# An expert mixture between attention and a gated feed-forward: row-number transfers and the widening of 64-bit weights take other places

## Chip, cores and metric

The kernel runs on one core of a Trainium2 chip. The metric is the time of one execution in device microseconds; three runs of the kernel before are given.

## Reference

The output is three stages, one behind the other, all in single precision (two of the weight arrays of the third stage arrive as 64-bit floats, because their set-up divides by a 64-bit square root).

```python
def reference(q, k, v, w_gate, w1, w2, x2_gate, x2_val, x2_out, rms_g):
    x = causal_attention(q, k, v)          # 2 x 12 heads, 448 x 64 each
    x = x.reshape(896, 768)                # tokens x model
    # 8 experts with room for 112 tokens each; token-expert pairs are taken
    # in the order of falling logits x @ w_gate until every token has a place
    for e in range(8):
        h = np.maximum(x[mask_e] @ w1[e], 0.0)     # 768 -> 1024
        y[mask_e] = h @ w2[e]                      # 1024 -> 768
    rms = np.sqrt(np.mean(y * y, axis=-1, keepdims=True) + 1e-06)
    xn = y / rms * rms_g
    g = xn @ x2_gate                               # 768 -> 1536
    return (g / (1 + np.exp(-g)) * (xn @ x2_val)) @ x2_out
```

## The kernel before, in words

Attention works head by head and leaves the tokens as rows of a DRAM tensor `xs`. Then come eight routing rounds, each of which fixes one expert and its 112 tokens (class `Round`), and eight expert iterations (class `Expert`), in which a routing round for a later expert is worked in between. Behind them stands the feed-forward stage, in 12 chunks of 128 hidden units (line 779), and the output product with the scatter to token order (lines 798 to 849).

**Order of the work.** The expert part is written out by hand: strings of two-letter words (`ITER`, `LASTR`, `END`), which `emit` turns into instructions. Inside `tc.manual_schedule` TensorE, ScalarE, VectorE and GpSimd each keep the order of these words. SP is not in that list, and neither are the instructions behind the block: a planner puts them where it takes their engine and buffers to be free, also between those of the block. In a round r the words mean:

- U0 to U7 and D0 to D7: the up and down matmuls of the expert with weight chunks 16r to 16r+15 (lines 656, 691); A: relu of half the hidden units (`hs`, ScalarE); T and H: their transposes and the copy `hf` on ScalarE (line 681)
- X0, X1: transposes of the gathered tokens of the next expert and the copies `xf` on ScalarE (line 609)
- N0, N1, N2: square (`sq`) and root on ScalarE, reciprocal on VectorE, and the scaled rows `yn` on VectorE (line 705), of the expert before; Y0, Y1: their transposes and the splits `xnh`, `xnl`
- Q2', F0', F1': the next expert's number goes to a register of SP (line 492), its row numbers `idx` are computed (line 508) and its tokens are gathered by an indirect transfer on GpSimd's queue (line 511)
- C: widening of half a block of 64-bit weights, 128 x 384, to single precision: one operation on ScalarE (line 527) and five on VectorE (531 to 535); J: its split into `hi` (ScalarE, 539) and `lo` (VectorE, 540)
- K0 to K7: the gate and value matmuls of feed-forward chunk 0 (line 551); S: its sigmoid-weighted unit

**Buffers and loads.** All weight loads go through SP's queue, 384 KB each. Expert chunk m lies in one of three rings of nine buffers, by m mod 3: "hi", "lo", "raw". The 64-bit loads (`load64`) take "raw" buffers, the split pairs `hi` and `lo` take those two rings. `g64` and `t64`, the scratch of the widening, have three buffers each. `split(n)` loads up to chunk n + 18; chunks of an expert can only be loaded once its number is in SP's register.

**The row numbers.** The output scatter (line 820) needs the row numbers `idx` in another layout, `idt`. They go to DRAM and back in two transfers of 896 elements of 4 bytes, issued from ScalarE's queue and written down behind the hand-ordered block (lines 760, 762). ScalarE's queue is in order.

Of the kernel before, what the change touches and what calls it, by code (L numbers as in the profile page):

```python
# [10 lines left out]
U32 = mybir.dt.uint32  # L11
# [9 lines left out]
NT = 7  # L21
D = 768
E = 8
CAP = N // E
F1 = 1024
# [12 lines left out]
AHEAD = 18  # L38
START0 = 'M0 M1 G G'
START1 = "G1' G' P0' P1' G' P2' P3' P4' G' P5' G1' P6' Q0' Q1' M1 O' G F0' F1' G P0 P1 Q2' G G G P2 P3 G X0 P4 P5 G X1 P6 U0+ Q0 U1+ U2+ Q1 U3+ U4+ O"  # L40
ITER0 = "Y1 A0 M1 N2 U5 G F0' G T0 U6 Q2' F1' H0 U7 Y0 G G G D0 N1 P0 P1 A1 P2 T1 D1 D2 D3 G H1 P3 D4 G X0 D5 P4 P5 P6 N0 D6 Q0 X1 D7"
ITER = "U0 Q1' U1 N0 N1 N2 U2 U3 Q2' A0 M1 Y0 U4 O' Y1 G U5 F0' T0 U6 F1' H0 U7 A1 G D0 G P0 G P1 T1 D1 D2 G P2 H1 P3 G D3 D4 G D5 P4 P5 D6 P6 X0 D7 Q0 X1"
LASTR = 'U0 U1 N0 N1 N2 U2 U3 A0 Y0 Y1 U4 T0 U5 U6 U7 H0 D0 A1 T1 D1 D2 H1 D3 C0 D4 C1 D5 D6 J0 C2 D7 J1 C3 K0'
PRE = 1
GVP = (128, 128, 128, 128)
END = 'N0 N1 N2 K1 J2 J3 Y0 Y1 S0 K2 K3 K4 K5 K6 S1 K7'
RACT = (0, 1)
QK = 'dd'
VH = 'a'
# [26 lines left out]
def tile_attn_moe_ffn(ctx, tc, qk, v, consts, wts, wgv, wout, rmsg, out):  # L76
    nc = tc.nc

    keep = ctx.enter_context(tc.tile_pool(name="keep", bufs=1))
# [4 lines left out]
    def bank(tag, name, bufs=2):  # L84
        return pools["ps"].tile([128, 512], F32, tag=tag, name=name, bufs=bufs)
# [5 lines left out]
    idxd = dram.tile([N, 1], U32, name="idxd")  # L91
# [276 lines left out]
    gone = rt1.tile([128, E], F32, name="gone")  # L368
    nc.gpsimd.memset(gone, 0.0)
    idx = keep.tile([CAP, E], U32, name="idx")  # L370

    def weave(*chains):
        chains = list(chains)
        while chains:
            chains = [c for c in chains if next(c, True) is None]

    class Round:
# [122 lines left out]
        def F(self, c):  # L500
            if c == 0:
                self.pi = bank("r", "pi")
                for t in range(NT):
                    nc.tensor.matmul(self.pi[:CAP, :2], self.o[:, t, :], ids[:, t, :], start=(t == 0),
                                     stop=(t == NT - 1))
                return
            rd = self.rd
            nc.vector.tensor_scalar(idx[:, rd:rd + 1], self.pi[:CAP, :1], self.pi[:CAP, 1:2], float(N - 1),
                                    op0=ALU.add, op1=ALU.min)
            xg = ex.tile([CAP, D], F32, tag="xg", name="xg", bufs=2)  # L510
            nc.gpsimd.indirect_dma_start(out=xg, out_offset=None, in_=xs,  # L511
                                         in_offset=bass.IndirectOffsetOnAxis(ap=idx[:, rd:rd + 1], axis=0))
            xgs.append(xg)

    evs, xgs, raws, ready = [], [], [], []

    def half64(src, j):
        return src[j // 4, j // 2 % 2, :, j % 2 * 384:j % 2 * 384 + 384]

    def load64(src):  # L520
        raw = ring.tile([128, 384, 2], U32, tag="raw", name="w64", bufs=NR)
        nc.sync.dma_start(out=raw, in_=src.bitcast(U32).rearrange("p (a b) -> p a b", b=2))
        return raw

    def widen(raw):
        g = cv.tile([128, 384], F32, tag="g64", name="g64", bufs=3)
        nc.scalar.activation(g, raw[:, :, 1].bitcast(F32), AF.Copy, scale=2.0 ** -112)  # L527
        gu = g.bitcast(U32)
        t = cv.tile([128, 384], U32, tag="t64", name="t64", bufs=3)
        x = t.bitcast(F32)  # L530
        nc.vector.tensor_scalar(t, gu, 3, None, op0=ALU.logical_shift_left)
        nc.vector.scalar_tensor_tensor(t, gu, 0x80000000, t, op0=ALU.bitwise_and, op1=ALU.bitwise_or)  # L532
        nc.vector.tensor_scalar(gu, t, 0xFF800000, None, op0=ALU.bitwise_and)
        nc.vector.scalar_tensor_tensor(g, raw[:, :, 0], 2.0 ** -52, g, op0=ALU.mult, op1=ALU.mult)  # L534
        nc.vector.tensor_add(x, x, g)  # L535
        return x
# [7 lines left out]
    def gate_val(half, which, dcs):  # L544
        c0 = half * S
        wh, wl = early[which]
        if (half, which) not in gv0:
            gv0[half, which] = bank("a" if half else "r", "pg")
        for dc in dcs:
            for n, (w, x) in enumerate(((wh, xnh), (wh, xnl), (wl, xnh))):  # L550
                nc.tensor.matmul(gv0[half, which][:, :S], w[:, dc * 128:dc * 128 + 128], x[:, dc, c0:c0 + S],  # L551
                                 start=(dc == 0 and n == 0), stop=(dc == 5 and n == 2))

    def tiles64():
        return (ring.tile([128, 768], F32R, tag="hi", name="hi", bufs=NH),
                ring.tile([128, 768], F32R, tag="lo", name="lo", bufs=NH))

    early, wide, raws64 = [], [], []

    def native(r, c):  # L560
        return c in FULL.get(r, FULL[-1])

    def load(n):
        while len(raws) <= min(n, 16 * len(evs) - 1):
            while len(raws64) < len(GVP) and GVP[len(raws64)] <= len(raws):
                raws64.append(load64(half64(wgv, len(raws64))))
            r, c = divmod(len(raws), 16)
            home = HOMES[len(raws) % len(HOMES)]
            raw = ring.tile([128, 768], F32, tag=home, name="raw", bufs=NR if home == "raw" else NH)
            nc.sync.dma_start(out=raw, in_=wts[bass.ds(evs[r], 1), c].rearrange("o p f -> (o p) f"))  # L570
            raws.append(raw)

    def split(n):
        load(n + AHEAD)
        while len(ready) <= min(n, len(raws) - 1, 16 * E - 1):
            r, c = divmod(len(ready), 16)
            raw = raws[len(ready)]
            if native(r, c):
                ready.append((raw, None))
                continue  # L580
            hi = ring.tile([128, 768], F32R, tag="hi", name="hi", bufs=NH)
            lo = ring.tile([128, 768], F32R, tag="lo", name="lo", bufs=NH)
            nc.scalar.copy(hi, raw)
            pool = c not in LOV.get(r, LOV[-1])
            (nc.gpsimd if pool else nc.vector).tensor_sub(lo, raw, hi.bitcast(F32))
            ready.append((hi, lo))
# [132 lines left out]
    def emit(words, r0):  # L719
        for w in words.split():  # L720
            op, c, r = w[0], int(w[1:].rstrip("'+") or 0), r0 + w.count("+")
            if op in "MGPQ" or op in "OF":
                k = r + 2 - (w[-1] == "'")
                if 0 <= k < E:
                    getattr(rounds[k], op)(c)
            elif op == "K":
                half, which, part = c // 4, c // 2 % 2, c % 2
                gate_val(half, which, range(3 * part, 3 * part + 3))
            elif op == "S":
                sg0[c] = cv.tile([128, S], F32, tag="sg", name="sg", bufs=2)  # L730
                nc.scalar.activation(sg0[c], gv0[c, 0][:, :S], AF.Silu)
            elif op == "C":
                while len(raws64) <= c:
                    raws64.append(load64(half64(wgv, len(raws64))))
                wide.append(widen(raws64[c]))
            elif op == "J":
                if c % 2 == 0:
                    early.append(tiles64())
                hi, lo = early[c // 2]
                c0 = c % 2 * 384  # L740
                halves(wide[c], hi[:, c0:c0 + 384], lo[:, c0:c0 + 384])
            elif op == "X":
                if r + 1 < E:
                    if c == 0 and r >= 0:
                        exps.append(Expert(r + 1))
                    getattr(exps[r + 1], op)(c)
            elif op in "NY":
                if r > 0:
                    getattr(exps[r - 1], op)(c)
            else:  # L750
                getattr(exps[r], op)(c)

    ET = mybir.EngineType
    with tc.manual_schedule(engines={ET.PE, ET.Activation, ET.DVE, ET.Pool}):
        emit(START0, -2)
        emit(START1, -1)
        for r in range(E):
            emit(ITER0 if r == 0 else LASTR if r == E - 1 else ITER, r)
        emit(END, E)
    nc.scalar.dma_start(out=idxd.rearrange("(e p) o -> p (e o)", p=CAP), in_=idx)  # L760
    idt = keep.tile([128, NT], U32, name="idt")
    nc.scalar.dma_start(out=idt, in_=idxd.rearrange("(t p) o -> p (t o)", p=128))

    ectx.close()
    with ExitStack() as fctx:
# [13 lines left out]
        for fc in range(NFC):  # L779
            gh, gl = early[2 * fc] if fc < PRE else pair64(wgv[fc, 0])  # L780
            vh, vl = early[2 * fc + 1] if fc < PRE else pair64(wgv[fc, 1])
            for half in range(2):
# [60 lines left out]
        for t, g in ((4, "d"), (5, "r"), (6, "c")):  # L843
            o = pair(g)
# [61 lines left out]
```

## Time and profile before

| What | Value |
|---|---|
| Median of three runs | 624.35 us (624.24, 624.35, 626.61) |
| Profiled execution, its time | 622.68 us |
| Profiled execution, its span | 620.9 us |
| TensorE busy | 584.1 us (94%) |
| VectorE busy | 410.9 us (66%) |
| ScalarE busy | 237.9 us (38%) |
| Mean granted clock of TensorE | 0.977 |

The profile is one execution; its span goes from the first instruction to the last, and 1.78 us of its time lie outside. PE stands for TensorE, PEld for its weight loads, DVE for VectorE, ACT for ScalarE, POOL for GpSimd and SP for the engine that issues the loads; a q behind a name is the engine's sequencer or queue. L760 is line 760 of the kernel. The granted clock is a share of 2.4 GHz. A matmul's end is modelled and overlaps the next one's start.

### The profile page before, as it was taken

To read this page: it belongs to the slowest core of one execution; us is meant where nothing else is said; L and a number is where in the kernel's file an instruction comes from. 1 tells how busy PE (TensorE), PEld (TensorE's weight loads), DVE (VectorE), ACT (ScalarE), POOL (GpSimd) and SP (SyncE) were. 2 spreads that over 40 slices of the span, in tenths; PEclk is the share of its full clock that TensorE was granted. 3 is DMA by queue.
4 is the path that set the end of the run, shared out by engine and by line. 5 is a ranking of instruction groups with operands and counts; after the bars stand their busy time and mean duration, and the time that the engine had idled before them with its cause. 6 is when DMAs were issued, how large, how long until landed. Compare 5 with 4: busy or idle time off the path is not lost.

```text
span 620.9 us, 9817 instructions
## 1 busy us (share of the span) xinstructions
PE 584.1 (94%) x3336; PEld 480.9 (77%) x3336; DVE 410.9 (66%) x1175; ACT 237.9 (38%) x575; POOL 109.5 (18%) x101
## 2 busy tenths in 40 slices
PE   4899999749999999999879899999999999999995
PEld 3899999636666666666445699999999999999995
DVE  7799999795454464544201999999999982991410
ACT  5799998301222131221212544334444333341200
POOL 4677884220020220202000000000000000000210
PEclk9999999958999999999998999999999999999999
DMA  9988971119995957859693544444445450100210
GB/s 275 268 254 255 257 217 33 30 46 383 355 322 209 365 195 272 298 189 369 238 272 99 179 125 160 149 132 122 154 153 153 120 151 11 51 2 1 101 42 35
DMA packets 49793, 109.26 MB, mean 176 GB/s; under 512 B 17056, under 2 KB 19232, under 8 KB 49744
## 3 DMA queue, kind: packets, MB, share of 16 engines
q1 hardware_dynamic: 45280, 93.96, 46.5%
q0 software_dynamic: 2640, 14.68, 7.4%
q8 instruction: 26, 0.43, 0.3%
q10 hardware_dynamic: 1824, 0.01, 0.2%
q14 instruction: 23, 0.19, 0.1%
HBM read 103.12 MB, written 5.51 MB: 175 GB/s over the span
## 4 chain that ended last, share of the span: by engine, by line
PE 85%; DMA 7%; DVE 3%; issue 2%; SPq 1%; ACT 1%; POOL 1%; POOLq 0%; ACTq 0%; DVEq 0%
PE hp L656 13%; PE pg L792 13%; PE pv L792 13%; PE o L813 12%; PE y L691 10%; PE sp L179 4%; PE pt L208 4%; PE ot L238 4%; PE pn L265 3%; DMA idxd<-idx 2%; PE pg L551 2%; DMA cs<-in_consts 2%; PE tp L600 2%; PE pc L426 1%; DMA raw<-in_wts 1%
## 5 line engine op out<-in xcount | busy, mean ns | idle before, releaser
L656 PE MATMUL hp<-raw,xf 128*112 128x512 f32 (+1 forms) x256 | 90.4, 502 | 4.0 <-ACT xf L609 3.8
L691 PE MATMUL y<-raw,hf 128*112 128x384 f32 x256 | 89.4, 490 | 2.7 <-ACT hf L681 2.7
L656 PEld LDWEIGHTS hp<-raw,xf 128*112 128x112 f32 x256 | 44.9, 183 | 33.3 <-issue 22.1
L691 PEld LDWEIGHTS y<-raw,hf 128*112 128x112 f32 x256 | 42.9, 177 | 33.9 <-issue 3.5
L820 POOL DMA_INDIRECT out<-ob,idt x7 | 6.8, 969 | 304.4 <-ACT ob L819 298.7
L200 ACT ACTIVATE pe<-sm,nm 128x256 f32<-128x256 f32 (+3 forms) x84 | 48.6, 581 | 2.5 <-DVE nm L190 2.1
L511 POOL DMA_INDIRECT xg<-xs,idx x8 | 21.5, 2687 | 156.9 <-DVE G L414 135.4
L539 ACT CAST hi<-t 128x384 fp32r<-128x384 f32 x58 | 29.5, 509 | 49.1 <-DVE t L535 48.9
L792 PE MATMUL pg<-xnl,hi 128*128 128x448 f32 x132 | 48.2, 365 | 0.0
L792 PE MATMUL pv<-xnh,lo 128*128 128x448 f32 x132 | 48.2, 365 | 0.0
L792 PE MATMUL pg<-xnh,hi 128*128 128x448 f32 x132 | 48.2, 365 | 0.0
L792 PE MATMUL pv<-xnh,hi 128*128 128x448 f32 x132 | 48.2, 365 | 0.0
L792 PE MATMUL pg<-xnh,lo 128*128 128x448 f32 x132 | 48.2, 365 | 0.0
L792 PE MATMUL pv<-xnl,hi 128*128 128x448 f32 x132 | 48.2, 365 | 0.0
L208 PE MATMUL pt<-cs,pe 128*128 128x128 f32 x228 | 41.3, 288 | 3.2 <-DVE ptl L225 2.6
L190 DVE CUSTOM_DVE_ANT_0 sm<-sp,mask 128x384 f32<-128x384 f32 (+3 forms) x84 | 42.2, 514 | 3.2 <-PE sp L179 2.3
L225 DVE TENSOR_TENSOR ptl<-pt,pth 128x512 fp32r<-128x512 f32 (+3 forms) x84 | 41.4, 514 | 2.5 <-ACT pth L221 2.5
L221 ACT CAST pth<-pt 128x512 fp32r<-128x512 f32 (+3 forms) x84 | 37.1, 445 | 10.3 <-PE pt L208 8.5
L527 ACT ACTIVATE g<-w 128x384 f32<-128x384 f32 x72 | 39.6, 554 | 0.6 <-DVE t L535 0.6
L179 PE MATMUL sp<-hi 128*128 128x384 f32 (+3 forms) x84 | 32.5, 397 | 6.9 <-DVE hi L165 5.5
L532 DVE SCALAR_TENSOR_TENSOR t<-g,t 128x384 uint32<-128x384 uint32 x72 | 38.3, 551 | 0.1
L534 DVE SCALAR_TENSOR_TENSOR g<-w,g 128x384 f32<-128x384 uint32 x72 | 38.2, 550 | 0.1
(149 smaller groups left out, 1239.9 us busy)
## 6 DMA issues: line engine op xcount, KB each, us to landing
raw<-in_wts SPq DMA_DIRECT2D x128, 384.0 KB, 7.8
w<-in_wgv SPq DMA_DIRECT2D x48, 384.0 KB, 3.5
w<-in_wout SPq DMA_DIRECT2D x24, 384.0 KB, 3.4
hi<-in_qk POOLq DMA_DIRECT2D x10, 896.0 KB, 6.2
qr<-in_qk SPq DMA_DIRECT2D x11, 448.0 KB, 5.6
vr<-in_v SPq DMA_DIRECT2D x12, 224.0 KB, 4.2
xs<-xl SPq DMA_DIRECT2D x12, 224.0 KB, 3.6
kr<-in_qk SPq DMA_DIRECT2D x10, 224.0 KB
```

The costliest lines, as they stand in the source:

```text
L179: nc.tensor.matmul(sp[:, :w], x[:, t * 128:t * 128 + 128], kh[:, w0:w0 + w], start=st, stop=not st)
L190: nc.vector.tensor_tensor_reduce(out=sm[:, :w], in0=sp[:, :w], in1=mask[:, MOFF[t]:MOFF[t] + w], op0=ALU.add, op1=ALU.min, scale=-0.125, s ...
L200: nc.scalar.activation(pe[:, :w], sm[:, :w], AF.Exp, bias=nm[:, t:t + 1], scale=-1.0, accum_out=sums[:, t:t + 1])
L208: nc.tensor.transpose(pt[:, b * 128:b * 128 + 128], pe[:, b * 128:b * 128 + 128], ident)
L225: nc.vector.tensor_sub(*rest.pop((h, t)))
L527: nc.scalar.activation(g, raw[:, :, 1].bitcast(F32), AF.Copy, scale=2.0 ** -112)
L532: nc.vector.scalar_tensor_tensor(t, gu, 0x80000000, t, op0=ALU.bitwise_and, op1=ALU.bitwise_or)
L534: nc.vector.scalar_tensor_tensor(g, raw[:, :, 0], 2.0 ** -52, g, op0=ALU.mult, op1=ALU.mult)
L656: nc.tensor.matmul(self.hp[:CAP, half, f0:f0 + n], a, b[:, o:o + n], start=(dc == 0 and i == 0), stop=(dc == 5 and i == len(ps) - 1))
L691: nc.tensor.matmul(self.ys[:CAP, u, :SQ], a, b[:, u * SQ:u * SQ + SQ], start=(c == 0 and i == 0), stop=(c == 7 and i == len(ps) - 1))
L792: nc.tensor.matmul(dst[:, :S], w[:, dc * 128:dc * 128 + 128], x[:, dc, c0:c0 + S], start=(dc == 0 and n == 0), stop=(dc == 5 and n == 2))
L813: nc.tensor.matmul(o[u][:, :SQ], x[:, fc % 6, :], w[:, u * SQ:u * SQ + SQ], start=(fc == 0 and n == 0), stop=(fc == NFC - 1 and n == 2))
```

## The change

The two row-number transfers are issued from GpSimd's queue, inside the hand-ordered block, right behind the gather of the last expert. A new word B issues one 64-bit load at its place; C no longer loads. Round 6 gets its own string, `ITER6`, with B0 to B3, C0, C1, J0, J1; the routing words that it leaves out do nothing in that round. `LASTR` (round 7) takes C2 to C7, J2 to J6 and B4 to B7, `END` J7. So gate and value weights of two chunks (`PRE = 2`, eight half blocks) are widened inside the block, where it was one (four half blocks). From chunk number 64 on (as n in `split`) loads are written down 11 chunks ahead where it was 18.

```diff
-LASTR = 'U0 U1 N0 N1 N2 U2 U3 A0 Y0 Y1 U4 T0 U5 U6 U7 H0 D0 A1 T1 D1 D2 H1 D3 C0 D4 C1 D5 D6 J0 C2 D7 J1 C3 K0'
-PRE = 1
-GVP = (128, 128, 128, 128)
-END = 'N0 N1 N2 K1 J2 J3 Y0 Y1 S0 K2 K3 K4 K5 K6 S1 K7'
+LASTR = 'U0 C2 B4 U1 N0 N1 N2 U2 U3 A0 Y0 Y1 U4 J2 B5 T0 U5 U6 C3 U7 H0 D0 A1 J3 B6 T1 D1 C4 B7 D2 H1 D3 J4 C5 D4 J5 D5 C6 D6 J6 D7 C7 K0'
+ITER6 = "U0 Q1' U1 N0 N1 N2 U2 U3 Q2' A0 B0 Y0 U4 O' Y1 U5 F0' B1 T0 U6 F1' H0 U7 A1 B2 D0 T1 D1 D2 H1 D3 C0 D4 D5 J0 C1 B3 D6 X0 D7 X1 J1"
+PRE = 2
+LATE = 64
+END = 'N0 N1 N2 K1 Y0 Y1 J7 S0 K2 K3 K4 K5 K6 S1 K7'
...
+    idt = keep.tile([128, NT], U32, name="idt")
...
             xgs.append(xg)
+            if rd == E - 1:
+                nc.gpsimd.dma_start(out=idxd.rearrange("(e p) o -> p (e o)", p=CAP), in_=idx)
+                nc.gpsimd.dma_start(out=idt, in_=idxd.rearrange("(t p) o -> p (t o)", p=128))
...
-            while len(raws64) < len(GVP) and GVP[len(raws64)] <= len(raws):
-                raws64.append(load64(half64(wgv, len(raws64))))
...
-        load(n + AHEAD)
+        load(n + (AHEAD if n < LATE else 11))
...
+            elif op == "B":
+                raws64.append(load64(half64(wgv, c)))
             elif op == "C":
-                while len(raws64) <= c:
-                    raws64.append(load64(half64(wgv, len(raws64))))
                 wide.append(widen(raws64[c]))
...
-            emit(ITER0 if r == 0 else LASTR if r == E - 1 else ITER, r)
+            emit(ITER0 if r == 0 else LASTR if r == E - 1 else ITER6 if r == E - 2 else ITER, r)
         emit(END, E)
-    nc.scalar.dma_start(out=idxd.rearrange("(e p) o -> p (e o)", p=CAP), in_=idx)
-    idt = keep.tile([128, NT], U32, name="idt")
-    nc.scalar.dma_start(out=idt, in_=idxd.rearrange("(t p) o -> p (t o)", p=128))
```

## Rows read from the trace of the kernel before

**Rows 1.** The page: the chain that ended last, shares by engine.

```profile
PE 85%; DMA 7%; DVE 3%; issue 2%; SPq 1%; ACT 1%; POOL 1%; POOLq 0%; ACTq 0%; DVEq 0%
```

**Rows 2.** Waits of TensorE, 290 to 400 us: total, times, longest.

```profile
PE hp L656 <- ACT xf L609: 3.8, 1, 3.8
PE y L691 <- ACT hf L681: 2.7, 1, 2.7
PE tp L600 <- DVE yn L705: 1.7, 1, 1.7
```

**Rows 3.** Chain of waits, 240 to 400 us: start, us, what.

```profile
301.62 7.28 DMA raw<-in_wts
...
308.98 15.19 DMA idxd<-idx
...
324.71 0.54 ACT xf L609
```

**Rows 4.** Timeline of ScalarE, 285 to 372 us: start, us, instruction, idle before.

```profile
311.94 0.53 ACT L681 COPY hf<-tp 128x448 f32<-128x448 f32 x1 [1.52 <-PE tp L669]
...
341.03 1.01 ACT L527 ACTIVATE g<-w 128x384 f32<-128x384 f32 x2
344.18 0.51 ACT L539 CAST hi<-t 128x384 fp32r<-128x384 f32 x1 [2.14 <-DVE t L535]
344.60 0.56 ACT L527 ACTIVATE g<-w 128x384 f32<-128x384 f32 x1
```

**Rows 5.** Timeline of TensorE, 290 to 400 us.

```profile
295.14 5.32 PE L656 MATMUL hp<-raw,xf 128*112 128x512 f32 x16
...
319.48 0.74 PE L600 MATMUL tp<-cs,xg 112*128 112x112 f32 x6
...
325.29 7.11 PE L656 MATMUL hp<-raw,xf 128*112 128x512 f32 x16 [3.78 <-ACT xf L609]
...
338.72 1.45 PE L691 MATMUL y<-raw,hf 128*112 128x384 f32 x4
...
349.14 0.66 PE L551 MATMUL pg<-xnh,hi 128*128 128x448 f32 x1
```

**Rows 6.** Timeline of VectorE, 293 to 372 us.

```profile
341.61 0.36 DVE L531 TENSOR_SCALAR t<-g 128x384 uint32<-128x384 uint32 x1 [7.21 <-ACT g L527]
...
343.59 0.56 DVE L535 TENSOR_TENSOR t<-t,g 128x384 f32<-128x384 f32 x1
...
349.89 0.62 DVE L531 TENSOR_SCALAR t<-g 128x384 uint32<-128x384 uint32 x2
...
352.84 0.55 DVE L535 TENSOR_TENSOR t<-t,g 128x384 f32<-128x384 f32 x1
...
353.84 1.01 DVE L705 SCALAR_TENSOR_TENSOR yn<-y,s,gb 112x768 f32<-112x768 f32 x1
```

**Rows 7.** Windows: length, busy by engine, clock, DMA share, GB/s.

```profile
315.00:320.00 5.00, 5.00 (x21) 2.92 (x20) 0.00 (x0) 0.00 (x0) 0.00 (x0) 1.00 1.06 200
...
325.00:330.00 5.00, 4.71 (x9) 2.49 (x10) 1.18 (x2) 1.58 (x5) 0.00 (x0) 0.66 0.48 119
...
420.00:500.00 80.00, 80.00 (x396) 74.15 (x395) 75.40 (x183) 32.24 (x69) 0.00 (x0) 1.00 0.46 139
```

**Rows 8.** Loads: issues by line with landing times, and DMA from 318 to 322.

```profile
L570 SPq DMA_DIRECT2D raw<-in_wts x10: 332/333/512, 298.7 to 304.6; - x10
...
DMA to landing us min/median/max: 3.1/9.9/10.9
...
L522 SPq DMA_DIRECT2D w<-in_wgv x9: 327/328/360, 315.5 to 343.6; - x9
...
DMA packets 173, 0.31 MB, mean 77 GB/s; under 512 B 73, under 2 KB 73, under 8 KB 173
q10 hardware_dynamic: 61, 0.00, 0.9%
```

**Rows 9.** The output scatters: ns min/median/max, first and last start.

```profile
L820 POOL DMA_INDIRECT out<-ob,idt x7: 959/962/1008, 575.4 to 616.0; - x7
```

## Prediction

> **What bounds the kernel now.** I read the page first: TensorE carries 85% of the chain that ended last [rows 1]. So the time is the sum of TensorE's work and its gaps, and the question is where gaps are left. The waits of TensorE between 290 and 400 us show only three, 3.78, 2.65 and 1.67 us [rows 2]. From 355 us on it never waits again, and the next thing to be seen at TensorE's side of the end is VectorE at 75.4 of 80 us in the middle of the feed-forward stage [rows 7]: nearly full, but ahead.
>
> The chain of waits says what the two larger gaps are [rows 3]. ScalarE's queue, in the sixth expert iteration (r = 6), meets the first row-number transfer. It stands until 308.9, when an earlier weight load lands (the chain has "raw<-in_wts" as what ends the wait). Then the second transfer waits 15.19 us for the first. In the first stop the copy `hf` (H0) is late and the first down matmul of r = 6 starts at 309.97 instead of 307.3, in the second the copy `xf` (X1) is late and round 7 starts at 325.29 instead of 321.5. The third gap, 353.2 to 354.91, has another cause: the scaling `yn` of the last expert (L705) stands on VectorE behind the widening operations of chunk C3, which run interleaved with those of a later chunk: C3's first operation at 349.89, its last at 352.84, `yn` only at 353.84 [rows 6].
>
> There is a fourth cost without a gap. Right after the 3.78 us gap the granted clock is 0.66 over 325 to 330 [rows 7], a stretch at the lower level, 1.2 GHz, inside it, and the 16 matmuls that open round 7 take 7.11 us where the same 16 took 5.32 in round 6 [rows 5]: 1.79 us lost.
>
> **The change, part by part.**
>
> *The two transfers go to GpSimd's queue, right behind the gather of the last expert.* GpSimd has nothing behind that gather until the first output scatter, whose issue is at 575.4 [rows 9]. So a wait of any length there is covered by some 270 us; without this cover it would be 15 us and more. ScalarE no longer stops. Gains: 2.65 + 3.78 = 6.43 us of gaps, and the 1.79 us of slow clock, because no gap is left in front of round 7: sum 8.22. Round 7 would start at 325.29 − 6.43 = 318.86.
>
> The transfer itself doesn't become cheaper: 3.5 KB in 896 pieces of 4 bytes went along with a collapse of the weight loads, 200 GB/s at a DMA share of 1.06 between 315 and 320 [rows 7], and 77 GB/s in its worst 4 us [rows 8]. The Trainium skill (page "Trainium Kernel Development and Optimization", Key Constraints) says that DMAs of the SP, ACT and POOL queues run on the same 16 engines and interleave, so that spreading them over queues saves only issue time. By that rule the collapse stays and the sum is the same 8.2 us, since it counts only ScalarE's stop; the trace agrees in that SP's loads slowed under a transfer from ScalarE's queue.
>
> *Loads B0 to B7.* They are the kernel's own loads, only earlier; each costs SP one issue of 0.33 us. B0 and B1 come among the weight loads of round 7 as number 1 and 7, B2 as number 10. In the trace the first ten issues lie from 298.7 to 304.6 and a load lands at most 10.9 us after its issue [rows 8]: B2 by 315.5, where its reader C2 is reached at 318.7. The seventh is issued near 302.6 and lands by 313.5; C1 is reached at 313.3, with 4 us in hand before `xf`. B3 is number 17; the load in that place was issued at 315.5 [rows 8], with 10.9 us it lands by 326.4, and C3 stands before H0, which is wanted at 330.5: some 3.5 us in hand. B4, number 21, lands near 330, C4 is reached at 331.6. Weights of round 7 are delayed by four loads, 1.57 MB or 8 us even at the 200 GB/s of 315 to 320 [rows 7]; the last is wanted some 20 us after the round's start, so this is hidden.
>
> *The shorter look-ahead (11 from chunk 60 on).* Weight loads wait for the expert number and for free buffers, which come in the same order, and SP issues them in that order; zero. With the B loads in the "raw" buffers, the load of chunk 125 waits for step D6 of round 6, which is 20 us before it is used. Zero.
>
> *Widening in round 6 (C0, J0, C1, J1).* VectorE has no instruction between the index and 326, so it is covered. One widening is five VectorE operations, 341.61 to 344.15, 2.54 us; ScalarE's cast follows at once, 0.42 later the next chunk's first operation starts on ScalarE, and VectorE follows 0.58 after that [rows 4, 6]. A link of the serial chain J, C thus costs 0.03 + 0.42 + 0.58 + 2.54 = 3.57 us. H1's copy, at 311.94 now [rows 4], moves 2.65 up to 309.3; C0 then widens by 312.8, C1 by 316.4. X0's transposes move from 319.48 [rows 5] to 316.8 and `xf` is wanted 0.6 behind, at 317.5. Not late. C2 follows behind `xf` and holds VectorE until 321.8, so `yn` of round 6 ends at 323.0; its transposes are wanted at 318.86 + 5.1 = 324.0. Cover of 1 us.
>
> *Widening in round 7 (C3 to C7).* Here I see the new wait. ScalarE reaches J3 and C4 only after A1, which needs the end of U7. D0 comes 13.43 us into round 7 now [rows 5], 11.64 without the slow clock: 330.5. A1, J3, C4 bring VectorE to C4 at 332.2. Four links: C4 ends at 334.75, C5 at 338.3, C6 at 341.9, C7 at 345.45. Behind C7 on VectorE stand the reciprocal and `yn`, 0.27 + 1.02 more: 346.7. TensorE reaches its gate matmuls 349.14 − 325.29 − 1.79 = 22.06 us into the round, 340.92, has 4.10 us of them (K0, K1; 349.14 to 353.24), and wants `yn` at 345.0. It waits 1.7 us, as before: the third gap stays, with another cause.
>
> It may grow. Widenings of the stage behind are put between these steps where their buffers are free. C3, interleaved, took 349.89 to 353.4, 3.5 us instead of 2.54, and its path to the start of `yn` 3.95 instead of 2.73 [rows 6]. The three scratch buffers come free for such a stranger after J5 and after J6, so C6 and C7 can be hit: 0.95 + 1.2 = 2.15 us. Bounds: 0 and 2.15; I take 1.2, one hit, which is the row that I have.
>
> *After 347 us* TensorE's work is the same and in the same order. Chunks 0 and 1 are ready by then; chunk 2 is wanted some 26 us later and needs four widenings. VectorE starts its work 30 us earlier and TensorE only 7, so it stays ahead. Zero.
>
> **Sum.** 8.22 − 1.2 = 7.0 us. The profiled execution took 622.68 (span 620.9 and 1.78 around it), so 615.7. The median of the runs is 624.35, 1.67 above it; on that scale 617.3.
>
> **The rivals.**
>
> *The third gap goes too.* If ScalarE gets through J5 to C7 before the last down matmul, `yn` is at once ready: 8.22 + 1.67 = 9.9, 614.5. Against it: the 3.57 us link, four times in 13 us.
>
> *The third gap draws the slow clock.* The gap of 2.65 us cost no clock, that of 3.78 did. With both hits the new gap is 1.7 + 2.15 = 3.9 us, and a slow stretch like the one of 325 us follows: 8.22 − 2.15 − 1.8 = 4.3, 620.1.
>
> *The gain is lost to late loads, no change.* C2 stands before `sq`, C3 before H0, all on ScalarE. If loads land 5 us or more later than reckoned, the covers above are used up and each further us is a us of TensorE; 9 to 12 us late leaves 0 to 3 us of gain, 622.5. For it: the collapse of 315 to 320 hits B3. Against: the last loads before landed within 10.9 us through that very collapse.
>
> *Slower: the index pieces jam the loads.* In the worst 4 us, 61 index packets passed and 77 GB/s [rows 8]. At that rate 896 pieces take 59 us. Some 11 loads of 0.39 MB, 4.3 MB, would be behind them: 56 us, chunk 127 lands at 313 + 56 = 369, wanted at 339.5; 30 − 7 = 23 us slower, 647. It decides from a jam of 28 us on, at that rate (then the loads end at 346.5, 7 us late); the whole transfer took 15.19 before. The Trainium skill (page "DMA: Bandwidth & Descriptors", Specifications) gives 512 bytes as the least size for line rate, below which the engines read and write back. By that rule the jam belongs to the pieces, whichever queue carries them; the 77 GB/s beside 61 packets agree.
>
> **How the numbers follow.** Forecast (gain 5.5 to 8.2) 0.62; third gap gone 0.12; slow clock there 0.11; late loads 0.10; jam 0.05. Half a per cent, 3.1 us, is about what a measurement here can tell. The first three are faster, 0.85; late loads the same, 0.10; the jam slower, 0.05. The range leaves out the last two: 613.9 to 621.0, with the third gap gone at one end and the slow clock at the other.
>
> **What would show it.** Right: no idle time before D0 of round 6 and U0 of round 7, round 7 at 319, its first 16 matmuls in 5.3 us, both transfers on GpSimd's queue; one gap of 2 to 4 us, released by VectorE's `yn`, some 26 us into round 7. Wrong: ScalarE waiting for `w<-in_wgv` ahead of `sq`, `hf` or `xf`; a low clock at 319 or behind the last gap; weight loads that take over 15 us; a TensorE wait after 360.

## The result and the profile after

The changed kernel takes 616.93 us (median of 4, 614.86 to 617.01), the kernel before in the same session 624.3 (624.01 to 626.61): ratio 0.9866, interval 0.9835 to 0.9897. In two later sessions, each timed against the kernel before, the ratio was nearer to 1: 0.9974 (0.9945 to 1.0004, so no gain clear of noise) and 0.9946 (0.9912 to 0.9979). Why is part of what the experiments found.

The profiled execution took 617.01 us, span 615.2. It is later than the one of before by 1.09 us when round 6 begins (counted from 0, the seventh of eight; 296.23 against 295.14, [rows 5]), a difference of which 0.84 is there by the first matmul of the first round (142.40 against 141.56), ahead of all that the change touches. So the two are compared from the start of round 6: 325.76 us from there to the end of the span before, 319.0 after, 6.8 less.

TensorE's waits of after, 290 to 400 us (total, times, longest), against the three of [rows 2]:

```profile
PE tp L603 <- DVE yn L708: 3.0, 1, 3.0
PE tp L603 <- DMA xg<-xs,idx: 0.3, 1, 0.3
```

The two gaps that ScalarE caused are gone. The gap in front of the last transposes is still there and has grown from 1.67 to 3.00 us. TensorE's timeline of after, for [rows 5]:

```profile
296.23 5.32 PE L659 MATMUL hp<-raw,xf 128*112 128x512 f32 x16
...
308.25 1.45 PE L694 MATMUL y<-raw,hf 128*112 128x384 f32 x4
...
318.10 0.77 PE L603 MATMUL tp<-cs,xg 112*128 112x112 f32 x6 [0.27 <-DMA xg<-xs,idx]
...
320.00 5.32 PE L659 MATMUL hp<-raw,xf 128*112 128x512 f32 x16
...
331.65 1.45 PE L694 MATMUL y<-raw,hf 128*112 128x384 f32 x4
...
342.06 0.66 PE L556 MATMUL pg<-xnh,hi 128*128 128x448 f32 x1
...
349.16 0.80 PE L603 MATMUL tp<-cs,yn 112*128 112x112 f32 x6 [3.00 <-DVE yn L708]
```

Round 6 starts at 296.23 and round 7 at 320.00: 23.77 us, where it was 30.15. The 16 matmuls that open round 7 take 5.32 us like those of round 6: no slow clock. From there to the last transposes it is 29.16 us, 29.62 before; from those to the end of the span 266.07, 265.99 before. So 6.38 of the 6.8 us are gained in the first of the three stretches. In the second the slow clock that is gone (1.79 us) is nearly eaten up by the growth of the last gap (1.33), which leaves 0.46.

GpSimd's timeline of after: start, length, and the idle time in front with its releaser.

```profile
305.92 0.92 POOL L513 DMA_INDIRECT xg<-xs,idx  x1 [21.47 <-DVE idx L510]
306.85 0.90 POOL L517 DMA_DIRECT2D idxd<-idx  x1
320.09 0.99 POOL L518 DMA_DIRECT2D idt<-idxd  x1 [12.34 <-DMA idxd<-idx]
```

The 12 us that one transfer waits for the other are spent on GpSimd now, where nobody stands behind. The DMA issues of after between 303 and 325 us (kind, count, size, median us to landing) show what the pieces do meanwhile:

```profile
raw<-in_wts SPq DMA_DIRECT2D x11, 384.0 KB, 14.9
...
xg<-xs,idx POOLq DMA_INDIRECT x1, 12.0
idxd<-idx POOLq DMA_DIRECT2D x1, 3.5 KB, 13.0
```

ScalarE's timeline of after shows two waits for 64-bit loads, at C2 and at C3:

```profile
320.62 0.55 ACT L532 ACTIVATE g<-w 128x384 f32<-128x384 f32 x1 [0.71 <-DMA w<-in_wgv]
...
327.92 0.55 ACT L532 ACTIVATE g<-w 128x384 f32<-128x384 f32 x1 [0.88 <-DMA w<-in_wgv]
```

VectorE's timeline of after, from the widening of C5 to `yn`:

```profile
336.94 0.35 DVE L536 TENSOR_SCALAR t<-g 128x384 uint32<-128x384 uint32 x1
...
340.51 0.35 DVE L536 TENSOR_SCALAR t<-g 128x384 uint32<-128x384 uint32 x1
...
344.09 0.35 DVE L536 TENSOR_SCALAR t<-g 128x384 uint32<-128x384 uint32 x1
...
345.35 0.35 DVE L536 TENSOR_SCALAR t<-g 128x384 uint32<-128x384 uint32 x1
...
346.09 0.35 DVE L536 TENSOR_SCALAR t<-g 128x384 uint32<-128x384 uint32 x1
346.36 0.55 DVE L537 SCALAR_TENSOR_TENSOR t<-g,t 128x384 uint32<-128x384 uint32 x1
346.83 0.55 DVE L540 TENSOR_TENSOR t<-t,g 128x384 f32<-128x384 f32 x1
347.30 0.16 DVE L705 RECIPROCAL s<-s 112x1 f32<-112x1 f32 x1
...
348.09 1.01 DVE L708 SCALAR_TENSOR_TENSOR yn<-y,s,gb 112x768 f32<-112x768 f32 x1
```

C5, C6 and C7 begin at 336.94, 340.51 and 344.09: links of 3.57 us. At 345.35 and at 346.09 two widenings of the stage behind begin in the midst of C7. From C7's start to the start of `yn` it is 4.00 us.

### The profile page after: what moved, and what is told of

The parts are those of the page before. It is cut to its first block, busy times and chain, and to the rows that moved or that the text cites. A ratio compares the mean times of both kernels' runs of the same rounds, so it can differ in the third digit from the quotient of the medians.

```text
span 615.2 us, 9821 instructions
## 1 busy us (share of the span) xinstructions
PE 584.0 (95%) x3336; PEld 481.6 (78%) x3336; DVE 413.0 (67%) x1175; ACT 238.7 (39%) x575; POOL 111.9 (18%) x103
## 4 chain that ended last, share of the span: by engine, by line
PE 86%; DMA 5%; DVE 3%; issue 2%; ACT 1%; SPq 1%; POOL 1%; POOLq 0%; ACTq 0%; DVEq 0%
PE hp L659 13%; PE pv L792 13%; PE pg L792 13%; PE o L813 12%; PE y L694 10%; PE sp L180 4%; PE ot L239 4%; PE pt L209 4%; PE pn L266 3%; DMA xg<-xs,idx 3%; PE pg L556 2%; DMA cs<-in_consts 2%; PE tp L603 2%; PE pc L428 1%; PE mr L407 1%
## 5 line engine op out<-in xcount | busy, mean ns | idle before, releaser
L659 PE MATMUL hp<-raw,xf 128*112 128x512 f32 (+1 forms) x256 | 88.9, 495 | 0.2
L545 DVE TENSOR_TENSOR lo<-t,hi 128x384 fp32r<-128x384 f32 x58 | 31.9, 556 | 16.0 <-ACT hi L544 16.0
```

What stands on the lines that cost most here:

```text
L659: nc.tensor.matmul(self.hp[:CAP, half, f0:f0 + n], a, b[:, o:o + n], start=(dc == 0 and i == 0), stop=(dc == 5 and i == len(ps) - 1))
```

## The experiments

The theory A of the expectations is that of the prediction: ScalarE's stop behind the row-number transfers is the whole gain, and the earlier widening adds nothing but keeps the third gap. Each expectation states its rivals itself. Where an execution starts late, its whole trace is shifted, so the column that tells most is the time from the first matmul of round 6 to that of round 7, from there to the last transposes (Y0) and from those to the end of the span, each a difference of two starts in TensorE's timeline of the profiled execution (in 9 two more groups of matmuls stand in front of Y0, so its last two columns don't compare with the others). The ratio is the one on record, with its interval; it is not the quotient of the two medians.

| kernel | median us (range, runs) | ratio to before (interval) | r6 to r7 | r7 to Y0 | Y0 to end |
|---|---|---|---|---|---|
| before | 624.3 (624.01 to 626.61, 4) | | 30.15 | 29.62 | 265.99 |
| changed | 616.93 (614.86 to 617.01, 4) | 0.9866 (0.9835 to 0.9897) | 23.77 | 29.16 | 266.07 |
| 1 transfers only | 614.57 (613.79 to 615.56, 6) | 0.9893 (0.9852 to 0.9934) | 23.31 | 27.83 | 266.08 |
| 2 widening only | 624.51 (622.45 to 627.83, 12) | 1.0052 (1.0025 to 1.0078) | 28.01 | 30.75 | 267.41 |
| 3 C7 behind Y1 | 613.8 (612.32 to 617.43, 6) | 0.988 (0.9838 to 0.9923) | 23.31 | 26.10 | 269.45 |
| 4 C6, J6, C7 behind Y1 | 614.02 (612.89 to 615.57, 6) | 0.9887 (0.9845 to 0.9929) | 23.31 | 26.00 | 267.30 |
| 5 changed again | 619.74 (614.82 to 623.16, 12) | 0.9974 (0.9945 to 1.0004) | 23.30 | 29.17 | 266.06 |
| 6 look-ahead 18 | 624.78 (622.81 to 632.32, 12) | 1.0048 (1.0013 to 1.0083) | 27.71 | 32.45 | 267.65 |
| 7 transfers at the end | 620.67 (614.37 to 623.41, 12) | 0.9956 (0.9917 to 0.9995) | 23.31 | 29.16 | 268.84 |
| 8 both 3 and 7 | 613.15 (612.55 to 615.11, 6) | 0.9869 (0.9832 to 0.9906) | 23.30 | 26.10 | 266.09 |
| 9 K2, K3 ahead of Y0 | 616.18 (614.09 to 618.09, 6) | 0.9889 (0.9852 to 0.9926) | 23.31 | 29.65 | 263.72 |
| 10 changed, third time | 619.51 (614.86 to 623.48, 12) | 0.9946 (0.9912 to 0.9979) | 23.31 | 29.15 | 272.17 |
| 11 transfers only, again | 616.84 (614.27 to 619.53, 7) | 0.9904 (0.9865 to 0.9943) | 23.31 | 27.83 | 266.08 |
| 12 ScalarE, at the end | 618.92 (616.4 to 624.0, 12) | 0.995 (0.9922 to 0.9979) | 23.31 | 29.16 | 265.97 |

1 to 4 ran together (before there 621.35), 5 to 8 together (622.13), 9 to 12 together (621.33).

**1. The transfers alone.** The kernel before, with the two transfers on GpSimd and nothing else changed.

```diff
             xgs.append(xg)
+            if rd == E - 1:
+                nc.gpsimd.dma_start(out=idxd.rearrange("(e p) o -> p (e o)", p=CAP), in_=idx)
+                nc.gpsimd.dma_start(out=idt, in_=idxd.rearrange("(t p) o -> p (t o)", p=128))
...
-    nc.scalar.dma_start(out=idxd.rearrange("(e p) o -> p (e o)", p=CAP), in_=idx)
-    nc.scalar.dma_start(out=idt, in_=idxd.rearrange("(t p) o -> p (t o)", p=128))
```

> The kernel before with one edit: the two row-number transfers issued from GpSimd's queue behind the last gather; all loads and widenings stay where they were. Theory A (ScalarE's stop is the whole gain): no gap before D0 of round 6 and U0 of round 7, the first 16 matmuls of round 7 in 5.3 us, the third gap unchanged at 1.7 us: 8.2 us faster than before, about 1.3 us faster than the changed kernel, ratio near 0.987. Rival B (the earlier widening brings the gain, since VectorE is then further ahead): no more than 3 us faster, ratio 0.995 to 1.

From round 6 to the end it takes 317.23 us, 8.5 less than before. Its waits of TensorE between 290 and 400 us are one, the third gap at its old size:

```profile
PE tp L604 <- DVE yn L709: 1.7, 1, 1.7
```

So the transfers alone bring the gain, and 1.8 us more of it than the whole change: 1.33 by what the third gap grew there (3.00 − 1.67), the rest in the stretch to round 7 (23.31 for 23.77; when the changed kernel ran again, as 5, it was 23.30). The same kernel was run once more, as number 11:

> The kernel before with the transfers alone moved, again, on this chip. Its third gap is 1.7 us and drew no slow stretch: 1.3 us below the best of the changed kernel's executions, spread below 3 us, so 2 to 5 us below the changed kernel's median.

Its stretches are the same to 0.01 us, and its median is 2.7 us below that of the changed kernel in the same session (10). Its executions spread over 5.3 us, not below 3.

**2. The widening alone.** The changed kernel with the transfers back on ScalarE's queue, written behind the block as before.

```diff
-            if rd == E - 1:
-                nc.gpsimd.dma_start(out=idxd.rearrange("(e p) o -> p (e o)", p=CAP), in_=idx)
-                nc.gpsimd.dma_start(out=idt, in_=idxd.rearrange("(t p) o -> p (t o)", p=128))
...
         emit(END, E)
+    nc.scalar.dma_start(out=idxd.rearrange("(e p) o -> p (e o)", p=CAP), in_=idx)
+    idt = keep.tile([128, NT], U32, name="idt")
+    nc.scalar.dma_start(out=idt, in_=idxd.rearrange("(t p) o -> p (t o)", p=128))
```

> The changed kernel with the two transfers put back behind the hand-ordered block on ScalarE's queue; loads, widening and look-ahead as changed. Theory A: the planner again puts them into round 6, ScalarE stops there, the gaps before D0 and U0 come back (some 6 us with the slow clock 8 us) and the third gap of 3.0 stays or shrinks because TensorE is later: 622 to 627 us, no gain over before. Rival B: still near 617.

TensorE's waits, 290 to 400 us, and ScalarE's timeline of this kernel:

```profile
PE hp L655 <- ACT xf L608: 4.0, 1, 4.0
PE tp L599 <- DVE yn L704: 3.0, 1, 3.0
PE y L690 <- ACT hf L680: 0.3, 1, 0.3
```

```profile
309.40 0.36 ACTq L759 DMA_DIRECT2D idxd<-idx  x1
...
323.89 0.40 ACTq L761 DMA_DIRECT2D idt<-idxd  x1
324.48 0.51 ACT L540 CAST hi<-t 128x384 fp32r<-128x384 f32 x1 [11.14 <-DMA w<-in_wgv]
```

ScalarE stands for 11 us again and the copy `xf` behind it is 4.0 us late; the third gap is 3.0. The row of the cast names a 64-bit load, but the second transfer is issued just before it, and the first, issued at 309.40, took 14.4 us to land: ScalarE stood at the transfers. The time is a little over that of before (1.0025 to 1.0078). The widening half by itself gains nothing.

**3 and 4. C7, or C6 and C7, behind the last transposes.** The changed kernel with C7 moved past Y1 in the written order, as shown; kernel 4 takes C6 and J6 out of the first line too and has Y1 C6 J6 C7 J7 in the second.

```diff
-LASTR = 'U0 C2 B4 U1 N0 N1 N2 U2 U3 A0 Y0 Y1 U4 J2 B5 T0 U5 U6 C3 U7 H0 D0 A1 J3 B6 T1 D1 C4 B7 D2 H1 D3 J4 C5 D4 J5 D5 C6 D6 J6 D7 C7 K0'
+LASTR = 'U0 C2 B4 U1 N0 N1 N2 U2 U3 A0 Y0 Y1 U4 J2 B5 T0 U5 U6 C3 U7 H0 D0 A1 J3 B6 T1 D1 C4 B7 D2 H1 D3 J4 C5 D4 J5 D5 C6 D6 J6 D7 K0'
...
-END = 'N0 N1 N2 K1 Y0 Y1 J7 S0 K2 K3 K4 K5 K6 S1 K7'
+END = 'N0 N1 N2 K1 Y0 Y1 C7 J7 S0 K2 K3 K4 K5 K6 S1 K7'
```

> The changed kernel with C7 moved from the end of round 7 behind Y1. If the third gap of 3.0 us is the chain J6, C7 and the later chunks' widenings mixed in, yn finds VectorE free: the reciprocal starts near 344.8 instead of 347.3, yn ends near 346.0 and TensorE wants it at 346.2: the gap goes to below 0.5 us, 3 us faster than the changed kernel, about 614. Rival: the gap is set by TensorE, ScalarE or the square of the last expert, not by VectorE's queue: it stays above 2 us and the time near 617.

> The changed kernel with C6, J6 and C7 moved behind Y1. By the same theory the gap is gone here too, and if the chain had been longer than reckoned more than in the run before it: 613.5 to 614.5. If the value weights of chunk 1 then come too late, TensorE waits near 364 us and the time goes up again; by the 3.57 us link they are ready near 358, so no wait.

In 3 no wait of TensorE is left between 290 and 400 us, and Y0 comes 26.10 us after the start of round 7, 3.06 sooner. C7 in front of `yn` is the third gap. Moving C6 too (4) gains only 0.1 more there and costs a wait for the sigmoid-weighted unit behind it, where the expectation had no wait:

```profile
PE pv L792 <- ACT sg L734: 1.0, 1, 1.0
```

Kernel 3's profiled execution was its slowest (617.43): it lost 3.4 us behind Y0, all over the feed-forward stage. The window of 420 to 500 us in this kernel (columns as in [rows 7]) has 389 matmuls in 80 us where after has 397, at the same granted clock of 1.00:

```profile
420.00:500.00 80.00, 80.00 (x389) 72.66 (x388) 73.87 (x177) 32.03 (x67) 0.00 (x0) 1.00 0.51 142
```

That is 205.7 ns a matmul for 201.5; times the 792 matmuls of that line group 3.3 us. Kernel 10, whose text is that of the changed kernel, has the same 389 there, so the order of C7 isn't its cause.

**5 and 10. The changed kernel again**, beside the other experiments, with no edit.

> The changed kernel itself, once more, beside the next three on one chip. From the start of round 6 to the end 319 us, third gap 3.0 us, time 1.1 to 1.3% below the kernel before.

> The changed kernel a third time, beside the run without the gap. By the theory its executions lie some in one group near 615 (gap of 3.0 without a slow stretch) and some 2 to 5 us above; median 616 to 620.

The gain of 1.1 to 1.3% that was expected of 5 didn't come. Both medians are some 3 us above the first, while the kernel before was 2 to 3 us faster in these sessions than in the first. The traces show one way in which that comes about. Windows behind the third gap, in kernel 5 and then in kernel 10 (granted clock third from the end):

```profile
350.00:355.00 5.00, 5.00 (x27) 4.63 (x26) 4.23 (x12) 2.36 (x6) 0.00 (x0) 1.00 0.25 96
```

```profile
345.00:350.00 5.00, 2.00 (x11) 1.55 (x10) 4.96 (x13) 1.83 (x6) 0.00 (x0) 0.88 0.33 114
350.00:355.00 5.00, 5.00 (x17) 4.52 (x16) 3.82 (x10) 4.40 (x9) 0.00 (x0) 0.50 0.48 157
355.00:360.00 5.00, 5.00 (x25) 4.53 (x24) 5.00 (x13) 0.36 (x1) 0.00 (x0) 0.94 0.12 17
```

The gap is 3.0 us in both. In 10 the granted clock is at 1.2 GHz for (0.12 + 0.50 + 0.06) × 2 × 5 = 6.8 us, from 348.8 on. TensorE works again from 349.53, so some 6.0 us of work go at half the clock and 3.0 us are lost: 17 matmuls in 5 us where 27 run in the other. Together with the slower pace of the matmuls, as in 3, that is about the 6.1 us by which its stretch from Y0 to the end is longer. Of the 28 timed executions of this kernel in the three sessions, the 12 with a mean granted clock of 0.977 or more have a median of 616.6 us, the other 16 (0.967 to 0.974) one of 621.1. Of the 24 executions of kernels 3, 4, 8 and 9, which have no third gap, 23 had 0.976 or more. That fits a slow stretch behind the gap in about half of the executions of the changed kernel; those that were only timed have no trace that would show where it lay. The mean alone doesn't tell it: kernel 11's profiled execution has 0.972 from a lower clock in its first 60 us (0.94 there) and runs at 1.00 behind its gap of 1.7 us. But of the 13 executions of kernels 1 and 11 it is the only one below 0.975.

**6. The look-ahead of 18 kept to the end.**

```diff
-LATE = 64
+LATE = 1000
```

> The changed kernel with the look-ahead of 18 in all rounds. If the shorter look-ahead costs or brings nothing by itself but only leaves room for B0 to B3 between the weight loads: those loads then come up to 7 places later in SP's queue, C1 or C2 on ScalarE waits for its load and xf or the square behind it is late by 0 to 4 us, so the same to 4 us slower than the changed kernel. Rival: no change within 1 us, since a load lands in time anyway.

TensorE's waits between 290 and 400 us, and ScalarE's timeline, of this kernel:

```profile
PE tp L603 <- DVE yn L708: 4.7, 2, 3.0
PE hp L659 <- ACT xf L612: 4.2, 1, 4.2
```

```profile
321.91 0.54 ACT L532 ACTIVATE g<-w 128x384 f32<-128x384 f32 x1 [8.71 <-DMA w<-in_wgv]
322.36 0.76 ACT L612 COPY xf<-tp 128x448 f32<-128x448 f32 x2
```

SP now issues more weight loads ahead of B1, C1 waits 8.7 us for it on ScalarE, and `xf` behind C1 is late. The whole gain is lost, and more than the 4 us expected at most: 5.0 by the medians beside 5. The 4.2 us gap draws a slow stretch (7.03 us for the 16 matmuls of round 7), and `yn` of round 6 is 1.7 us late too. This is the rival of the late loads, and the shorter look-ahead is what keeps it away.

**7. The transfers at the end of the block.** VectorE copies the row numbers behind the last step, and GpSimd transfers the copy.

```diff
         emit(END, E)
+        idx2 = keep.tile([CAP, E], U32, name="idx2")
+        nc.vector.tensor_copy(idx2, idx)
+        nc.gpsimd.dma_start(out=idxd.rearrange("(e p) o -> p (e o)", p=CAP), in_=idx2)
+        nc.gpsimd.dma_start(out=idt, in_=idxd.rearrange("(t p) o -> p (t o)", p=128))
```

> The changed kernel with the two transfers behind the hand-ordered block: VectorE copies the row numbers there and GpSimd's queue sends the copy, so that no 4-byte piece is under way in rounds 6 and 7. If the pieces are what slows the loads: the window 310 to 320 has above 300 GB/s where it had about 200, the last gather lands within 9 us, no wait of TensorE on it, C2 and C3 don't wait for loads; about 0.3 us gained, so the time is the same within 0.5 us. Rival: the gather and the loads are as late without the pieces, because the extra 64-bit loads fill the queue.

Windows of after, and then of this kernel (the last column is GB/s):

```profile
310.00:315.00 5.00, 5.00 (x17) 2.76 (x17) 3.15 (x7) 1.95 (x4) 0.00 (x0) 1.00 1.21 221
315.00:320.00 5.00, 4.73 (x19) 2.58 (x18) 2.17 (x6) 1.19 (x3) 0.00 (x0) 1.00 0.89 176
```

```profile
310.00:315.00 5.00, 5.00 (x20) 2.81 (x19) 1.09 (x3) 1.58 (x3) 0.00 (x0) 1.00 1.03 359
315.00:320.00 5.00, 5.00 (x17) 2.72 (x16) 4.17 (x9) 0.97 (x2) 0.00 (x0) 1.00 1.03 385
...
350.00:355.00 5.00, 3.60 (x13) 3.34 (x14) 4.87 (x12) 2.73 (x6) 0.00 (x0) 0.55 0.51 169
```

Without the pieces the loads run at 359 and 385 GB/s in these windows, with them at 221 and 176. (Round 6 begins 2.7 us later in this execution; in 12, which also has no pieces there and begins round 6 within 0.03 us of after, the two windows have 356 and 401.) The time doesn't show it: the stretch to round 7 is 23.31 us, as in 5 with the pieces (23.30). The third gap stays at 3.0 us, and in this execution too a slow stretch follows it; the stretch behind Y0 is 2.8 us longer, and the median 0.9 us above that of 5.

**8. Experiments 3 and 7 together.**

> Both: C7 behind Y1 and the transfers behind the block. No wait of TensorE of 0.3 us or more between 290 us and the end; from the start of round 6 to the end 315.5 us, 3.3 us less than the changed kernel, 1.6 to 1.8% below the kernel before. Rival: something else takes up the time, as in the profile with C7 alone behind, where the stage after 346 us took 3.4 us longer: then it is near the changed kernel.

TensorE has no wait at all between 150 and 600 us, no slow stretch follows, and the three stretches sum to 315.5 us, 10.3 less than before. At 613.15 us it has the lowest median of the study (3 and 4, run in another session, lie within 0.9 us of it), and its executions lie within 2.6 us. The 315.5 us were expected; the gain of 1.6 to 1.8% lies at the far end of the one measured, 1.3% (0.9 to 1.7).

**9. Two chunks' gate matmuls more ahead of Y0**, to fill the third gap with work rather than to remove its cause.

```diff
-END = 'N0 N1 N2 K1 Y0 Y1 J7 S0 K2 K3 K4 K5 K6 S1 K7'
+END = 'N0 N1 N2 K1 K2 K3 Y0 Y1 J7 S0 K4 K5 K6 S1 K7'
```

> The changed kernel with K2 and K3 ahead of Y0, so that TensorE has 3.65 us of gate and value matmuls to do while it waits for yn; VectorE and ScalarE keep their order. If the gap in front of yn's transposes is what makes the executions of the changed kernel differ (614.8 to 623.2), through the clock behind it: no gap, no slow stretch at 350 us, spread below 4 us and median 612 to 614. Rival (the spread comes from elsewhere): only the 3.0 us go, the median falls by 3 and the spread stays 8 us.

The gap is gone. A smaller one comes in its place, behind the transposes instead of before them; it is the only wait between 290 and 400 us:

```profile
PE pg L556 <- DVE xnl L615: 1.1, 1, 1.1
```

From round 6 to the end it takes 316.68 us, 2.3 less than the changed kernel, and no slow stretch follows. The median of 616.18 misses the 612 to 614 expected, while the spread falls to 4.0 us from the 8 of the changed kernel: the gap is a part of that spread, but the theory doesn't account for the whole time.

**12. The transfers on ScalarE's queue, but at the end of the block.**

```diff
         emit(END, E)
+        nc.scalar.dma_start(out=idxd.rearrange("(e p) o -> p (e o)", p=CAP), in_=idx)
+        nc.scalar.dma_start(out=idt, in_=idxd.rearrange("(t p) o -> p (t o)", p=128))
```

> The changed kernel with the two transfers on ScalarE's queue, but written at the end of the hand-ordered block. This parts the queue from the place. If ScalarE's stop costs only where a copy that TensorE needs stands behind it: rounds 6 and 7 as in the changed kernel, ScalarE stops near 355 us for 5 to 12 us, where casts and one sigmoid unit stand behind it; chunk 2 is wanted only near 372, so 0 to 3 us slower than the changed kernel. Rival (the queue itself is the cost): 6 us or more slower.

ScalarE's timeline of kernel 12:

```profile
359.93 0.36 ACTq L760 DMA_DIRECT2D idxd<-idx  x1
...
371.28 0.39 ACTq L761 DMA_DIRECT2D idt<-idxd  x1
371.71 0.51 ACT L541 CAST hi<-t 128x384 fp32r<-128x384 f32 x1 [9.52 <-DMA idxd<-idx]
```

ScalarE stops for 9.5 us there too, and TensorE loses nothing: the chunks are widened far enough ahead. What the change cures is the place of the stop, not the queue.

## Why the prediction was right

The time, 616.93 us, is 0.4 from the 617.3 predicted, and the gain from round 6 on 6.8 us where the sum said 7.0. That the first median came so near is in part luck: its four executions all had a mean granted clock of 0.977 or more, of the 24 later ones only eight, and in the two later sessions the medians of the changed kernel lie only 2.4 and 1.8 us below those of the kernel before, where they lay 7.4 us apart in the first. What bears the sum out is its steps, read from the traces:

- **ScalarE's stop, 6.43 us of gaps.** Measured 30.15 − 23.77 = 6.38, and shown to be the transfers' by 1 (with them alone moved the gain is there) and 2 (with them left in place it isn't). Where the gather isn't late the stretch is 23.31, so the stop had cost 6.84, a little more than its gaps.
- **The slow clock, 1.79 us.** Round 7 opens with 5.32 us for the 16 matmuls, as in round 6; no slow stretch lies there in any profile in which `xf` is in time.
- **The third gap, 2.9 us.** It is 3.00. The links of 3.57 us are there one by one, K0 comes 342.06 − 320.00 = 22.06 us into the round as reckoned, and of C6 and C7 only C7 is hit, as was taken: 4.00 us from C7's start to `yn` are 1.28 more than the 2.72 of C2, which is not hit in this trace, for the 1.2 reckoned. That the size fits is partly luck: the row behind the 1.2 has operations of one later widening in between, C7 here those of two. That C7 is the cause is shown by 3, which moves it and loses the gap.
- **The loads, in hand by 3 to 4 us.** Mis-sized, and covered by what stood elsewhere. The 10.9 us to landing, the most in [rows 8], became a median of 14.9 in after and up to 16.4; without the pieces beside them it is 7.8 in 7 and 9.2 in 12. ScalarE waited 0.71 us for B2 in front of `sq` and 0.88 us for B3 in front of `hf`, and `yn` of round 6 ended 0.2 us before its transposes were due, for the 1 us reckoned. TensorE saw none of it. So two of the signs by which the prediction was to be wrong did come, loads of over 15 us and these waits, but the cover held.
- **The gather, not treated as late.** Its 12.0 us to landing (9.1 in kernel 5) made the 0.27 us wait. Small, but not in the sum.
- **The shorter look-ahead, zero.** True of its own cost: the stretch to round 7 is 23.30 us in 5 and 23.31 in 1, which keeps 18. (The step says chunk 60; the change begins at 64.) It missed that the loads' margin hangs on it: with 18 the kernel takes some 9 us more from round 6 to the end (327.8 for 319.0).
- **The jam of the pieces.** The rate fell to about half, and the first transfer took 13.0 us, far from the 59 us that the worst stretch would have made. The Trainium skill ("DMA: Bandwidth & Descriptors", Specifications) gives 512 bytes as the least size for line rate; the trace agrees, 3.5 KB in pieces of 4 bytes took 13.0 us to land. That the loads beside them slow down is shown by 7 and 12, where they recover when the pieces go elsewhere.
- **The slow clock at the third gap, 0.11.** Too small a chance. With 3.0 us of gap it came in kernels 2, 6, 7 and 10 and stayed away in after, 5 and 12. The prediction wanted 3.9 us for it, and named a low clock behind the last gap as a sign of being wrong. It is a likely reason for the higher later medians of the changed kernel, 619.7 and 619.5, which are still within the range; the trace of 10 shows it for one execution.

So the change gains by one of its halves. The other half, the earlier widening, takes 1.3 us back in every profile and up to some 3 us more in those where the clock falls. Once C7 leaves the path of `yn` (8) the stretch from round 6 to the end is 1.7 us shorter than with the transfers alone (315.5 for 317.2); whether moving C3 behind Y1 in the old order would close that gap of 1.7 us as well, without the earlier widening, was not run.

Open are four things: what decides whether the 3.0 us gap draws the lower clock (2, 7 and 10, where it did, also had a granted clock of 0.94 in their first 60 us, 6 had 0.97 there, and after, 5 and 12, where it didn't, 0.97 to 1.00; that the two belong together is not shown); why some executions run the feed-forward matmuls 2% slower at full granted clock (3 and 10, some 3 us); why the kernel before, of which there is only one profile, was 2 to 3 us faster in the later sessions; and the differences of up to 3.8 us that arise before the first expert round (its first matmul lies at 141.3 in 5 and at 145.1 in 7).

## What to carry to other kernels

On an in-order queue look for a transfer whose result is wanted late and see who stands behind it: here it could go behind the urgent work on ScalarE's own queue (12) or to GpSimd's, and its wait of 9.5 to 12.3 us there cost TensorE nothing. Work that is brought forward off the critical path must not come ahead of a small operation on it; moving one step behind that operation, or giving the waiting engine other work, took the gap away. A gap that lowers the clock in some executions and not in others can make the times scatter, so one trace of such a kernel says too little: repeat it, and close the gap.

## What the runs showed of the hardware

- A transfer of 3.5 KB in 896 pieces of 4 bytes cut the loads beside it from 359 and 385 GB/s (7) or 356 and 401 (12) to 221 and 176 (after), while the DMA share stayed near 1 (1.21 and 0.89 against 1.03).
- Idle TensorE time of 1.7 us never drew the lower clock in these traces; 3.0 us did in four of seven profiles, 3.8 to 4.2 us in front of round 7 did in each of the three profiles that have it (before, 2 and 6).
- The same matmuls at a granted clock of 1.00 went at about 201.5 ns in twelve of the fourteen profiles and at 205.7 ns in two (3 and 10).
